# Wide products by S, ten ReLU halves on ScalarE, and a new hand-written order in an attention-then-routing kernel

## The chip, the cores and the metric

The kernel runs on one core of one Trainium2 chip. The metric is the device time of the whole launch in microseconds. The core has a matrix engine (PE, with its weight loads shown apart as PEld), a vector engine (DVE), a scalar engine (ACT) and GpSimd (POOL). Each runs its own queue in order. SP issues most of the DMAs, and POOL issues the indirect ones (scatters by a list of row numbers).

## What is computed

Two blocks are joined. The first is an attention without softmax. For each of 4 x 4 batch-heads, with 1088 rows of 32 numbers each, q and k are projected by two 8 x 32 matrices S1 and S2, and the outer product of the two projections (64 numbers) is the feature vector of the row. The second sends each of the 4352 resulting rows of 128 numbers to one of 8 experts.

```
def phi(x):
    a = np.einsum('rd,bhsd->bhsr', S1, x)
    b = np.einsum('rd,bhsd->bhsr', S2, x)
    return np.einsum('bhsi,bhsj->bhsij', a, b).reshape(*x.shape[:-1], r * r)
q_p, k_p = (phi(q), phi(k))
kv = np.einsum('bhsf,bhsd->bhfd', k_p, v)
z = np.sum(k_p, axis=2)
num = np.einsum('bhsf,bhfd->bhsd', q_p, kv)
den = np.einsum('bhsf,bhf->bhs', q_p, z)[..., None] + 1e-06
attn = num / den
...
x = attn.transpose(0, 2, 1, 3).reshape(B * S, H * D)
logits = x @ w_gate
expert_idx = np.argmax(logits, axis=1)
...
for e in range(E):
    mask = expert_idx == e
    h = np.maximum(x[mask] @ w1[e], 0.0)
    out[mask] = gate_w[mask, None] * (h @ w2[e])
```

S1 and S2 come as 64-bit floats. The kernel splits each of their numbers into a high and a low 32-bit part (`s_cat[:, 0]` and `s_cat[:, 1]`), so the projection is the sum of a product by the high part and a product by the low part.

## The kernel before, in words

All arithmetic of the large products is in fp32. The work is written as small named operations, each issuing instructions for mostly one engine, and one string, `ORDER`, lists them: every engine runs its instructions in the order in which this list names them. After the list a loop at the end of the kernel does the tiles that it leaves over. Buffers are handed out from rings while the list is walked, so the list also sets which buffer an operation reuses and whom it waits for.

The attention is cut into chunks of 512 rows of one batch: `k00`, `k01` ... `k31` for k (batch, chunk), `q00` ... `q31` for q, and `kr0`, `kr1`, `qr0`, `qr1` for the remainders (one quarter of the size). A chunk's operations are:

- `.t` four transposes on PE, `.x` ACT copies them out of PSUM, `.a` PE multiplies by S (L359), `.s` ACT copies the projections out of PSUM in another order (L368), `.o` DVE forms the outer products (L378, 128 x 1024 numbers).
- for k: `.v` PE adds the chunk to kv (L387, L391).
- for q: `.T` and `.U` PE transposes the features, `.c` and `.d` ACT copies them, `.n` and `.N` PE multiplies them by kvx (L505, 128 x 82), and DVE divides: `.e`, `.g`, `.y` for the first half of the chunk and `.e2`, `.g2`, `.y2` for the second. `.g` gives logits, `.y` gives rows of x.

`e0` ... `e3` end a batch's kv: `.r` adds the remainder, `.k`, `.t`, `.c`, `.m`, `.z` turn kv into kvx, which the batch's `.n` needs. `r0` ... `r3` route a batch: `.a`, `.b`, `.c`, `.d` on DVE (argmax and ranks, a small PE step `.p` between `.b` and `.d`), and then the scatters `.s0` ... `.s8` on POOL, each of which writes 128 rows into `xs_dram` at their places, sorted by expert. `t0`, `t1` and `t2` compute on DVE which expert and which rows the tiles 0 to 9, 10 to 17 and 18 onwards hold.

A tile `j0`, `j1`, ... is 128 rows of one expert: `.l` SP loads the rows, `.x` PE transposes them, `.c` ACT copies the result, `.w` DVE copies the expert's first weights into a buffer of the `wide` ring (L832), `.u` and `.U` PE multiplies by the two halves of them (L837, 8 instructions each), `.r` ACT does the ReLU of the first half (L854) and `.q` DVE that of the second (L860), `.d` PE multiplies by the second weights (L869, 16 instructions), `.y` ACT scales, `.s` POOL scatters the rows to the output. Tiles 0 to 9 may be loaded once the scatters of batches 0 and 1 have landed, tiles 10 to 17 once those of batch 2 have, the rest after batch 3. In this run 37 tiles are computed: 34 always, and 3 of the 7 that stand under conditions near the end.

Of the kernel before, what the change touches and what calls it, by code (L numbers as in the profile page):

```python
# [12 lines left out]
AF = mybir.ActivationFunctionType  # L13
ALU = mybir.AluOpType
# [3 lines left out]


ORDER = """  # L20
k00.t k00.x k01.t S.t k01.x S.m k00.a kr0.t k01.a k00.s kr0.x k00.o kr0.a k01.s kr0.s kr0.o k00.v k01.o q00.t
q01.t q00.x k01.v q01.x k10.t q01.a k10.x k10.a q01.s q01.o k11.t k10.s q00.a k11.x k10.o k11.a q00.s q00.o
k10.v k11.s e0.r q01.U e0.k k11.o q00.U q01.d e0.t q00.d q00.T e0.m e0.c e0.z q01.T q00.c q00.N q01.c q01.N
q00.e2 q00.y2 q01.n q00.g2 q01.e2 q01.g2 q01.y2 q00.n q01.e q01.y k21.t q00.e k11.v q01.g k21.x q00.g q00.y
q11.t r0.a k21.a q11.x r0.b r0.x q11.a k21.s r0.c e1.r k21.o q11.s qr0.t r0.p e1.k qr0.x q11.o e1.t qr0.a e1.c
q10.t qr0.s e1.m r0.d k20.t q10.x q11.T k20.x q10.a e1.z r0.s2 qr0.o q11.c q11.U q10.s qr0.T r0.s1 q10.o q11.d
q11.n qr0.c q11.N q11.e r0.s6 q11.g q11.y q10.T q11.e2 q10.U q10.c q11.y2 qr0.n r0.s4 q11.g2 q10.d q10.n qr0.e
qr0.y r0.s7 q10.N qr0.g q10.e q10.y q21.t q10.g q10.e2 k20.a r0.s5 q21.x q10.g2 q10.y2 r1.a q21.a k20.s r0.s0
k30.t k20.o r1.x q21.s q20.t k30.x kr1.t k31.t r0.s3 q20.x r1.b k30.a k31.x r1.c r1.p q21.o k30.s kr1.x q20.a
r1.d q21.T k30.o q20.s r1.s8 q21.U q21.c k20.v q21.d q20.o k30.v r1.s1 k21.v t0.a k31.a r1.s2 t0.b q20.T k31.s  # L30
q20.U q20.c k31.o kr1.a r1.s5 q30.t q20.d qr1.t q31.t kr1.s q30.x t0.c k31.v qr1.x r1.s0 q31.x kr1.o q30.a
j0.w e2.r r1.s3 q30.s qr1.a j1.w e2.k e3.r qr1.s e2.t e3.k j2.w q31.a r1.s4 e2.c e2.m qr1.o e3.t q31.s e2.z
qr1.T q30.o r1.s6 e3.c q21.n qr1.c q20.n e3.m t0.d r1.s7 q21.e q20.N e3.z q21.g q21.y q20.e q21.N q31.o qr1.n
q20.y q30.T q20.e2 q30.U q21.e2 q30.c j3.l q20.y2 q31.T q21.g2 q30.d q21.y2 q30.n q20.g2 j0.l q31.c qr1.e
q20.g q30.N qr1.g r2.a j4.l q31.n q30.e r2.x j1.l r2.b q31.U r2.c r2.p q31.d j2.l q30.y q30.g j0.x q30.e2
q31.N j0.c r2.d j0.u q30.y2 r2.s2 t1.a j1.x j0.U j0.r q30.g2 t1.b j1.c r2.s7 j1.u j5.l j0.q j3.x t1.c j2.x
j1.r j0.d r2.s4 j3.c j3.w j2.c r2.s1 t1.d j1.U j0.y qr1.y q31.e j2.u j0.s q31.e2 j6.l j1.q j4.x j4.w j2.U j2.r
r2.s3 j4.c j1.d q31.y2 j7.l j5.w r2.s6 j2.q j5.x j3.u q31.g j1.y q31.g2 q31.y r2.s5 j5.c r3.a j2.d j3.r j1.s
r3.b r3.x r3.c r3.p j2.y r2.s0 j3.U r3.d j2.s j4.u j3.q j8.l j6.w j6.x j3.d j4.r r3.s7 j6.c t2.a r3.s1 j5.u
t2.b j3.y j4.U j5.r r3.s6 j6.u t2.c j9.l j7.x r3.s4 j5.U j6.r j4.q j7.c j6.U j10.l j5.q r3.s3 j7.w j4.d j11.l  # L40
j9.w r3.s5 j9.x j6.q j8.x j4.y j5.d j9.c r3.s0 j8.c j8.w t2.d r3.s8 j7.u j5.y j6.d j7.r r3.s2 j7.U j3.s j6.y
j8.u j12.l j7.q j6.s j10.w j10.x j7.d j8.r j10.c j4.s j9.u j7.y j5.s j8.U j9.r j9.U drain j13.l j8.q j11.w
j11.x j8.d j11.c j14.l j9.q j12.w j12.x j10.u j8.y j12.c j9.d j10.r j11.u j9.y j7.s j10.U j11.r j9.s j12.u
j13.w j15.l j13.x j11.U j12.r j10.q j8.s j13.c j12.U j14.w j16.l j13.u j12.q j17.l j11.q j14.x j15.x j13.U
j14.c j15.c j15.w j14.u j18.l j16.w j10.d j14.U j13.q j13.r j10.y j18.o j11.d
"""
AFTER_LATE = "k11.o"
PREPARE = (18, 19, 20, 21, 23, 24, 27)
# [6 lines left out]
def kernel(  # L55
# [21 lines left out]
    JC = 4  # L77
# [23 lines left out]
    def new(name, shape, dtype=FP):  # L101
        return sb.tile(shape, dtype, name=name)
# [14 lines left out]
    def ring(name, n, shape, dtype=FP):  # L117
        return Ring([new(f"{name}{i}", shape, dtype) for i in range(n)])
# [2 lines left out]
    wide = ring("wide", WIDE, [128, 1024])  # L121
    xT_bufs = ring("xT", 3, [128, 512])
    sum_bufs = ring("sum", 4, [128, 2 * JC * H * R])
    q_pT_bufs = ring("q_pT", 5, [128, 512])
    kvz_bufs = ring("kvz", 2, [128, 96])
    xg_bufs = ring("xg", 14, [128, XW])
    xgT_bufs = ring("xgT", 7, [128, 128])
    hTa_bufs = ring("hTa", 3, [128, HF])
    hTb_bufs = ring("hTb", 3, [128, HF])
    to_bufs = ring("to", 14, [128, 1], I32)  # L130
    y_bufs = ring("y", 12, [128, DM])
    xs_dram = dram.tile([(E + 1) * NTOK, XW], I32, name="xs_dram")


# [75 lines left out]
    for b in range(B):  # L210
        t = new(f"x_rows{b}", [128, J + 1, XW])
# [57 lines left out]
    s_cat = new("s_cat", [128, 2, 2, 4, R])  # L269
# [41 lines left out]
    def hold(t, n):  # L311
        holders[id(t)] = [t, n]
# [26 lines left out]
    def features(x, n, srcs, take_dst, keeps):  # L339
        st = {}  # L340

        @op(x + ".t")
        def _():
            t = st["tp"] = banks.take()
            for i, s in enumerate(srcs()):
                nc.tensor.transpose(t[:, ts(i, 128)], in_=s, identity=ident)  # L346

        @op(x + ".x")
        def _():
            st["xT"] = xT_bufs.take()  # L350
            nc.scalar.copy(out=st["xT"][:, :n * 128], in_=st["tp"][:, :n * 128])  # L351
            banks.give(st["tp"])

        @op(x + ".a")
        def _():
            t = st["ab"] = banks.take()
            for i in range(n):
                for part in range(2):
                    nc.tensor.matmul(t[:, ts(i, 64)], lhsT=st["xT"][:, ts(i, 128)],  # L359
                                     rhs=s_cat[:, part].rearrange("p t g r -> p (t g r)"),  # L360
                                     start=(part == 0), stop=(part == 1), skip_group_check=True)
            xT_bufs.give(st["xT"])

        @op(x + ".s")
        def _():
            s = st["s"] = sum_bufs.take()
            hold(s, 1 + keeps)
            nc.scalar.copy(out=s[:, :n * 64].rearrange("p (g i r) -> p i g r", i=n, r=R),  # L368
                           in_=st["ab"][:, :n * 64].rearrange("p (i g r) -> p i g r", i=n, r=R))
            banks.give(st["ab"])  # L370

        @op(x + ".o")
        def _():
            s = st["s"]
            st["p"] = take_dst()
            dst = st["p"][:, :n * 4 * RR].rearrange("p (g a b) -> p g a b", a=R, b=R)
            a, b = (s[:, ts(t, n * 32)].rearrange("p (g r) -> p g r", r=R) for t in range(2))
            nc.vector.tensor_tensor(dst, a[:, :, :, None].broadcast_to([128, n * 4, R, R]),  # L378
                                    b[:, :, None, :].broadcast_to([128, n * 4, R, R]), ALU.mult)
            let(sum_bufs, s)  # L380

        return st
# [398 lines left out]
    st = [dict() for _ in range(JT)]  # L781
# [8 lines left out]
    def expert_tile(j):  # L790
        x = f"j{j}"
        s = st[j]

        @op(x + ".l")
        def _():
            s["xg"] = xg_bufs.take()
            r = word(tiles[j][1], [SP], E * NTOK)
            d = nc.sync.dma_start(out=s["xg"].bitcast(I32), in_=xs_dram[ds(r, 128), :])
            g = (j >= JE) + (j >= JF)
            if g not in begun:  # L800
                begun.add(g)
# [55 lines left out]
        @op(x + ".q")  # L857
        def _():
            s["hTb"] = hTb_bufs.take()
            nc.vector.tensor_scalar(s["hTb"], s["hb"], 0.0, None, ALU.max)  # L860
            banks.give(s["hb"])

        @op(x + ".d")
# [112 lines left out]
    def part(js, bit):  # L976
        for j in js:
            st[j]["y"] = y_bufs.take()
        with tc.If(bit > 0):
# [64 lines left out]
```

## Time and profile before

| what | us |
|---|---|
| median of 4 runs | 228.27 |
| runs | 228.01, 232.96, 228.53, 227.22 |
| the profiled execution's own time | 228.01 |
| its span, first to last instruction | 226.2 |
| PE busy / DVE busy / ACT busy / POOL busy | 215.9 / 120.6 / 73.0 / 82.5 |
| first product by S, first transpose of a tile, last product | 9.3, 79.04, 221.9 |

The run's time is 1.8 us longer than the span. In the profile a group is a line of the kernel, an engine and an operation, with its count, its busy time and the mean of one. A PE product's own duration (275 ns) is longer than the distance from one start to the next, because products overlap in the array: what PE can take in is read from the starts in the timeline. One fp32 product of the program is two PE instructions. A wait is put down to what came last.

### The profile page before, as it was taken

Reading aid. Unit: us, or ns where it says so; the run is one execution under the profiler, and the core shown is the slowest. Engines: PE = TensorE matmul, PEld = TensorE weight load, DVE = VectorE, ACT = ScalarE, POOL = GpSimd, SP = SyncE. Lnnn points to the kernel's source line nnn. Section 1 sums busy time; section 2 is a strip of 40 time slices with the busy share of each in tenths; the row PEclk is TensorE's granted clock in tenths of the full one; section 3 lists DMA queues with packets and bytes.
Section 4 is the critical chain, followed back from the end, with each engine's and each line's share of the span. In section 5 each row is a group of like instructions: output and inputs, shape, how many; then the busy total and the mean of one; then the engine's idle time right before and its main releaser. Section 6 shows DMA issues by size and latency. Waiting matters only on the chain. (4 is left out here: it accounts for less than half of the span.)

```text
span 226.2 us, 6247 instructions
## 1 busy us (share of the span) xinstructions
PE 215.9 (95%) x2245; PEld 211.6 (94%) x2245; DVE 120.6 (53%) x389; ACT 73.0 (32%) x190; POOL 82.5 (36%) x103
## 2 busy tenths in 40 slices
PE   6999999999999999997999999999999699999992
PEld 5889999999999999997999999999999699999991
DVE  4244678587678999989652422425344343323220
ACT  2243524524452332331323222332323223132320
POOL 5100000871781056777615033222222234117133
PEclk9999999999999999999999999999999999999998
DMA  5999999998112211152121112111010110000000
GB/s 163 286 348 247 251 297 345 337 346 264 45 46 60 64 47 47 61 118 63 47 61 35 35 38 59 39 35 51 15 44 26 47 33 16 10 3 32 25 25 15
DMA packets 29279, 23.33 MB, mean 103 GB/s; under 512 B 5866, under 2 KB 27116, under 8 KB 29248
## 3 DMA queue, kind: packets, MB, share of 16 engines
q1 hardware_dynamic: 26304, 18.15, 28.8%
q0 software_dynamic: 2400, 4.50, 5.6%
q8 instruction: 20, 0.33, 0.6%
q10 hardware_dynamic: 544, 0.26, 0.4%
q14 instruction: 11, 0.09, 0.1%
HBM read 17.81 MB, written 5.55 MB: 103 GB/s over the span
## 5 line engine op out<-in xcount | busy, mean ns | idle before, releaser
L837 PE MATMUL bank<-xgT,wide 128*128 128x128 f32 x592 | 72.2, 275 | 0.0
L837 PEld LDWEIGHTS bank<-xgT,wide 128*128 128x128 f32 x592 | 69.1, 192 | 0.0
L860 DVE TENSOR_SCALAR hTb<-bank 128x512 f32<-128x512 f32 x37 | 25.3, 688 | 67.3 <-PE bank L837 54.6
L616 POOL DMA_INDIRECT xs_dram<-x_rows,row_i x34 | 37.7, 1107 | 55.6 <-DVE kvx L467 29.1
L869 PE MATMUL bank<-w_all,hTb 128*128 x296 | 39.3, 276 | 1.2 <-DVE hTb L860 1.2
L883 POOL DMA_INDIRECT out_dram<-y,to x23 | 23.0, 1000 | 47.5 <-ACT xgT L825 32.8
L869 PE MATMUL bank<-w_all,hTa 128*128 x296 | 39.3, 276 | 0.0
L869 PEld LDWEIGHTS bank<-w_all,hTb 128*128 128x128 f32 x296 | 36.0, 192 | 1.4 <-DVE hTb L860 1.4
L869 PEld LDWEIGHTS bank<-w_all,hTa 128*128 128x128 f32 x296 | 36.0, 192 | 0.2
L878 ACT ACTIVATE y<-bank,xg 128x128 f32<-128x128 f32 x37 | 13.6, 367 | 65.9 <-PE bank L869 65.9
L359 PE MATMUL bank<-s_cat,xT 128*128 128x64 f32 x272 | 32.8, 275 | 0.4 <-DVE s_cat L332 0.4
L359 PEld LDWEIGHTS bank<-s_cat,xT 128*128 128x128 f32 x272 | 31.5, 192 | 0.9 <-issue 0.5
L854 ACT ACTIVATE hTa<-bank 128x512 f32<-128x512 f32 x37 | 22.1, 597 | 28.2 <-PE bank L837 22.6
L883 POOL DMA_INDIRECT out_dram<-y,xg x18 | 18.0, 1000 | 31.3 <-ACT y L878 17.9
L832 DVE COPY wide<-w_all 128x1024 f32 x39 | 27.2, 708 | 1.7 <-issue 1.6
L378 DVE TENSOR_TENSOR wide<-sum 128x1024 f32<-128x1024 f32 (+1 forms) x18 | 20.4, 1132 | 11.6 <-ACT sum L368 11.5
L505 PE MATMUL bank<-kvx,q_pT 128*128 128x82 f32 x128 | 15.4, 276 | 0.3 <-ACT q_pT L493 0.3
L505 PEld LDWEIGHTS bank<-kvx,q_pT 128*128 128x128 f32 x128 | 14.8, 192 | 0.6 <-ACT q_pT L493 0.5
L368 ACT COPY sum<-bank 128x256 f32<-128x256 f32 (+1 forms) x20 | 6.8, 341 | 24.7 <-PE bank L359 23.4
L351 ACT COPY xT<-bank 128x512 f32<-128x512 f32 (+1 forms) x20 | 9.9, 527 | 12.6 <-PE bank L346 11.5
L493 ACT COPY q_pT<-bank 128x512 f32<-128x512 f32 (+1 forms) x18 | 9.4, 566 | 7.3 <-PE bank L485 7.1
L825 ACT COPY xgT<-bank 128x128 f32<-128x128 f32 x41 | 10.0, 263 | 5.2 <-PE bank L820 4.9
(153 smaller groups left out, 160.6 us busy)
## 6 DMA issues: line engine op xcount, KB each, us to landing
w_all<-in_moe_w_dram SPq DMA_DIRECT2D x16, 512.0 KB, 8.7
xg<-xs_dram SPq DMA_DIRECT2D x41, 65.0 KB, 1.8
wide<-in_v_dram SPq DMA_DIRECT2D x4, 512.0 KB, 5.6
wide<-in_q_dram SPq DMA_DIRECT2D x4, 512.0 KB, 8.6
wide<-in_k_dram SPq DMA_DIRECT2D x3, 512.0 KB, 7.9
xs_dram<-fill SPq DMA_DIRECT2D x1, 585.0 KB, 11.0
xs_dram<-x_rows,row_i POOLq DMA_INDIRECT x34, 2.9
out_dram<-y,to POOLq DMA_INDIRECT x23, 2.2
```

The costliest lines, as they stand in the source:

```text
L359: nc.tensor.matmul(t[:, ts(i, 64)], lhsT=st["xT"][:, ts(i, 128)], rhs=s_cat[:, part].rearrange("p t g r -> p (t g r)"), start=(part == 0), ...
L378: nc.vector.tensor_tensor(dst, a[:, :, :, None].broadcast_to([128, n * 4, R, R]), b[:, :, None, :].broadcast_to([128, n * 4, R, R]), ALU.mult)
L505: nc.tensor.matmul(o, lhsT=lhsT, rhs=kvx[b][:, hp].rearrange("p g c -> p (g c)"), start=True, stop=True)
L616: d = nc.gpsimd.indirect_dma_start(out=xs_dram[:], out_offset=bass.IndirectOffsetOnAxis(ap=st["row"][:, u:u + 1], axis=0), in_=x_rows[b][: ...
L825: nc.scalar.copy(out=s["xT"], in_=s["tp"][:, :128])
L832: nc.vector.tensor_copy(out=s["w1"], in_=w1_all[:, ds(r, F)])
L837: nc.tensor.matmul(t[:, ts(c, 128)], lhsT=s["w1"][:, ts(c0 + c, 128)], rhs=s["xT"], start=True, stop=True)
L854: nc.scalar.activation(s["hTa"], s["ha"], AF.Relu)
L860: nc.vector.tensor_scalar(s["hTb"], s["hb"], 0.0, None, ALU.max)
L869: nc.tensor.matmul(t[:, :DM], lhsT=h[:, ts(c % 4, 128)], rhs=w2_all[:, ds(r + c * DM, DM)], start=(c == 0), stop=(c == 7))
L878: nc.scalar.activation(s["y"], s["py"][:, :DM], AF.Copy, bias=0.0, scale=s["xg"][:, DM:DM + 1])
L883: d = nc.gpsimd.indirect_dma_start(out=out[:], out_offset=bass.IndirectOffsetOnAxis(ap=s["to"](), axis=0), in_=s["y"], in_offset=None, bou ...
```

## The change

Four things change.

- `.a` multiplies each transposed block once by the high and low part side by side (128 columns) instead of twice by 64 columns with accumulation. The low half of the result goes to its own columns in PSUM.
- The two halves are added on DVE. A new operation `.l` of a chunk copies the low half out of PSUM on ACT into a buffer `lo`, of which there is one; `.s`, now on DVE, adds the high half from PSUM to it and writes the sum in the order that the ACT copy used before.
- `.q` is on ACT for tiles 0 to 9 (JE is 10), and on DVE for the others as before.
- `ORDER` is a new list. The rings `xg` and `y` have one buffer less each. The loop at the end, with its conditions, is as it was.

```diff
-    xg_bufs = ring("xg", 14, [128, XW])
+    lo_bufs = ring("lo", 1, [128, JC * H * 2 * R])
+    xg_bufs = ring("xg", 13, [128, XW])
...
-    y_bufs = ring("y", 12, [128, DM])
+    y_bufs = ring("y", 11, [128, DM])
...
             for i in range(n):
-                for part in range(2):
-                    nc.tensor.matmul(t[:, ts(i, 64)], lhsT=st["xT"][:, ts(i, 128)],
-                                     rhs=s_cat[:, part].rearrange("p t g r -> p (t g r)"),
-                                     start=(part == 0), stop=(part == 1), skip_group_check=True)
+                nc.tensor.matmul(t[:, ts(i, 128)], lhsT=st["xT"][:, ts(i, 128)],
+                                 rhs=s_cat.rearrange("p w t g r -> p (w t g r)"), start=True, stop=True)
             xT_bufs.give(st["xT"])
+
+        def part(i):
+            return st["ab"][:, :n * 128].rearrange("p (i w c) -> p i w c", i=n, w=2)[:, :, i]
+
+        @op(x + ".l")
+        def _():
+            st["lo"] = lo_bufs.take()
+            nc.scalar.copy(out=st["lo"][:, :n * 64].rearrange("p (i c) -> p i c", i=n), in_=part(1))
 
         @op(x + ".s")
         def _():
             s = st["s"] = sum_bufs.take()
             hold(s, 1 + keeps)
-            nc.scalar.copy(out=s[:, :n * 64].rearrange("p (g i r) -> p i g r", i=n, r=R),
-                           in_=st["ab"][:, :n * 64].rearrange("p (i g r) -> p i g r", i=n, r=R))
+            nc.vector.tensor_tensor(
+                s[:, :n * 64].rearrange("p (g i r) -> p i g r", i=n, r=R),
+                part(0).rearrange("p i (g r) -> p i g r", r=R),
+                st["lo"][:, :n * 64].rearrange("p (i g r) -> p i g r", i=n, r=R), ALU.add)
             banks.give(st["ab"])
+            lo_bufs.give(st["lo"])
...
             s["hTb"] = hTb_bufs.take()
-            nc.vector.tensor_scalar(s["hTb"], s["hb"], 0.0, None, ALU.max)
+            if j < JE:
+                nc.scalar.activation(s["hTb"], s["hb"], AF.Relu)
+            else:
+                nc.vector.tensor_scalar(s["hTb"], s["hb"], 0.0, None, ALU.max)
             banks.give(s["hb"])
```

Of the new list, the stretch around the first tile's load reads as follows (`...` leaves out what lies before and behind):

```
...
q21.g2 q21.g q21.y q30.U r1.s4 r1.s3 q31.d q31.N q20.g2 r2.a r2.b j1.w q30.d q31.n r1.s2 q31.e q31.g q31.y
q30.c j0.w qr1.n q30.N r2.p r1.s8 r1.s1 r2.d r2.x q31.e2 q31.y2 r1.s0 q31.g2 qr1.e qr1.g j0.l r2.c j0.x q30.n
j0.c j1.l j1.x j1.c r2.s3 j0.u j0.U j2.l j0.r r2.s5 j0.q j2.x j2.w r2.s2 qr1.y j3.l j3.x j3.c j4.l j2.c j1.u
...
```

and that in the list before:

```
...
q20.g q30.N qr1.g r2.a j4.l q31.n q30.e r2.x j1.l r2.b q31.U r2.c r2.p q31.d j2.l q30.y q30.g j0.x q30.e2
q31.N j0.c r2.d j0.u q30.y2 r2.s2 t1.a j1.x j0.U j0.r q30.g2 t1.b j1.c r2.s7 j1.u j5.l j0.q j3.x t1.c j2.x
...
```

More of the change, by code (lines that the diff above doesn't have):

```diff
@@ L20 @@
 ORDER = """
[L21 to L45, printed above, removed]
+k00.t k00.x k01.t S.t S.m k00.a kr0.t k01.x k00.l k00.s k00.o kr0.x k01.a k01.l k01.s kr0.a k01.o q01.t q01.x
@@ new lines @@
+q00.t k00.v kr0.l kr0.s kr0.o q00.x q01.a q01.l q01.s q01.o k11.t k11.x k01.v e0.r k10.t q00.a e0.k e0.t e0.m
+e0.z k10.x q00.l q00.s q00.o q10.t k10.a q10.x e0.c k11.a k10.l k10.s k10.o q01.T q01.c q10.a q10.l qr0.t
+q10.s q10.o q01.U q01.d q00.T q00.c q01.n q01.e k11.l q01.y q00.U k11.s q21.t q00.n q00.e qr0.x qr0.a k11.o
+q00.d q00.y q01.N qr0.l q00.N qr0.s q21.x q11.t q21.a k10.v k11.v q00.e2 e1.r q11.x q20.t q00.g2 qr0.o q21.l
+q01.e2 q01.g2 q01.g q00.g r0.a q21.s r0.x q11.a q10.U k20.t r0.b r0.p q01.y2 e1.k e1.t q00.y2 r0.c q11.l k20.x
@@ new lines @@
+q10.d qr0.T q11.s q11.o k20.a r0.d r0.s2 r0.s6 q20.x r0.s4 q10.T r0.s7 q11.U e1.c e1.m e1.z q11.T q21.o q10.N
+k20.l k20.s k20.o q10.e2 q10.c q10.n q10.y2 q11.c q10.e r0.s0 q10.g q11.n q11.e q11.g q10.g2 qr0.c qr0.n qr0.e
+r0.s1 qr0.g q11.d q11.N k21.t k21.x kr1.t q10.y kr1.x q11.e2 q11.g2 r1.a r1.b r0.s3 q11.y2 r1.x q20.a k30.t
+q20.l k20.v q30.t qr0.y r1.p q11.y r1.c kr1.a q30.x q20.s r1.d r1.s7 r1.s5 q20.o k30.x k21.a k21.l k21.s k31.t
+r0.s5 k21.o kr1.l k31.x kr1.s kr1.o q21.U q21.d q31.t qr1.t t0.a t0.b q30.a k30.a k30.l q31.x k30.s t0.c k30.o
@@ new lines @@
+k21.v e2.r e2.k qr1.x k31.a k31.l q20.U q20.d q21.T e2.t e2.m q31.a qr1.a e2.z k31.s k31.o q20.T e2.c q31.l
+q31.s q31.o r1.s6 q21.N q21.e2 q21.c q20.N qr1.l qr1.s qr1.o k30.v k31.v q20.e2 e3.r q20.y2 q20.c e3.k q31.T
+q31.U q21.y2 q30.l q30.s q20.n q31.c q30.o e3.t e3.c e3.m e3.z qr1.T qr1.c q21.n q20.e q20.g q30.T q20.y q21.e
+q21.g2 q21.g q21.y q30.U r1.s4 r1.s3 q31.d q31.N q20.g2 r2.a r2.b j1.w q30.d q31.n r1.s2 q31.e q31.g q31.y
+q30.c j0.w qr1.n q30.N r2.p r1.s8 r1.s1 r2.d r2.x q31.e2 q31.y2 r1.s0 q31.g2 qr1.e qr1.g j0.l r2.c j0.x q30.n
@@ new lines @@
+j0.c j1.l j1.x j1.c r2.s3 j0.u j0.U j2.l j0.r r2.s5 j0.q j2.x j2.w r2.s2 qr1.y j3.l j3.x j3.c j4.l j2.c j1.u
+j1.U j1.r j4.x j4.c j2.u j1.q q30.e2 j2.r q30.e j2.U j3.w j3.u j4.w j0.d j0.y j1.d j5.w q30.y q30.g j5.l j5.x
+q30.g2 r3.a r3.b j5.c j4.u j4.r j4.U j3.r j3.U j6.w j0.s t0.d t1.a t1.b j5.u t1.c r2.s4 j2.q j6.l j6.x r2.s6
+j7.w j1.y j1.s j3.q r2.s7 j2.d j3.d j5.r j5.U j8.l q30.y2 j8.x j8.w j6.c j6.u j3.y j3.s j6.U j7.l j9.w j7.x
+j4.q j4.d j5.q j9.l r2.s1 t1.d r2.s0 j10.l j6.q j9.x j7.c j7.u j7.U j9.c r3.x j2.y j11.l r3.p j5.d j6.r r3.c
@@ new lines @@
+j6.d r3.d t2.a j7.r j7.q t2.b j2.s r3.s1 r3.s7 j10.w j8.c j8.u j8.r j8.U j11.x j10.x j10.c t2.c j9.u j9.r t2.d
+j11.w j5.y r3.s5 j5.s j8.q j9.U j12.w j9.q j12.l j10.u j7.d r3.s4 j13.l j12.x j10.U j10.q j10.r j12.c j15.l
+j8.d j11.c j4.y j14.l j11.u j13.x j11.r j12.u j13.w j12.U j15.w j11.U j14.x r3.s2 j13.c j6.y j14.c j17.l j9.d
+j13.u j9.y j10.d j12.q j6.s r3.s3 j12.r j13.r r3.s0 drain j7.y j7.s j15.x j14.w j15.c j11.q j11.d j14.u j12.d
+j14.r j14.U j17.x j16.l j14.q j17.c j13.U j15.u j15.U r3.s8 r3.s6 j13.q j20.l j16.x j16.c j11.y j12.y j16.w
@@ L46 @@
+j11.s j13.d j13.y j15.r j14.d
 """
```

## The prediction

> **What bounds the kernel now.** I read the page's busy shares and groups first, then PE's waits, then the timelines of PE and DVE around the places that the change touches.
>
> ```profile
> PE 215.9 (95%) x2245; PEld 211.6 (94%) x2245; DVE 120.6 (53%) x389; ACT 73.0 (32%) x190; POOL 82.5 (36%) x103
> PE   6999999999999999997999999999999699999992
> DVE  4244678587678999989652422425344343323220
> L359 PE MATMUL bank<-s_cat,xT 128*128 128x64 f32 x272 | 32.8, 275 | 0.4 <-DVE s_cat L332 0.4
> L368 ACT COPY sum<-bank 128x256 f32<-128x256 f32 (+1 forms) x20 | 6.8, 341 | 24.7 <-PE bank L359 23.4
> ```
>
> PE is busy from end to end and waits for almost nothing; what it waits for by name is 6.4 us in all, the longest of it these three:
>
> ```profile
> PE bank L820 <- PEq L979: 1.7, 1, 1.7
> PE bank L869 <- DVE hTb L860: 1.2, 1, 1.2
> PE bank L224 <- DVE zeros L169: 1.1, 1, 1.1
> ```
>
> So a microsecond of PE work removed ahead of the last product is worth about one microsecond, if the other engines can follow. The second row of digits says where that is in doubt: DVE is at six to nine tenths in the stretch in which the products by S stand (9.3 to 69.3 us).
>
> What PE pays for one instruction is the distance between starts:
>
> ```profile
> 16.64 3.68 PE L359 MATMUL bank<-s_cat,xT 128*128 128x64 f32 x32
> 20.16 0.61 PE L346 MATMUL bank<-ident,wide 128*128 128x128 f32 x4
> ...
> 63.98 2.00 PE L359 MATMUL bank<-s_cat,xT 128*128 128x64 f32 x16
> 65.91 0.32 PE L387 MATMUL bank<-k_rem_p,v_rem 64*32 64x64 f32 x8
> ...
> 190.72 3.74 PE L837 MATMUL bank<-xgT,wide 128*128 128x128 f32 x32
> 194.29 1.06 PE L869 MATMUL bank<-w_all,hTa 128*128 x8
> ```
>
> 32 products of 64 columns take 20.16 - 16.64 = 3.52 us, 110 ns each; in the worse group 16 take 1.93, 121 ns. 32 of 128 columns take 194.29 - 190.72 = 3.57, 112 ns each. The width costs nothing between 64 and 128.
>
> **The change, part by part.** *The wide product.* 272 instructions become 136. Before: 272 x 110 to 272 x 121, 29.9 to 32.9; I take 114 (most groups lie at 110 to 114), 31.0. After: 136 x 112 = 15.2. PE loses 14.7 to 17.7 us of work; I take 15.5.
>
> The Trainium skill speaks against this one: "TensorE: Matmul & The Clock Gate", in the steps of Part 2, has a stream of matmuls cost one cycle per moving column, N/2.4 + 2.5 ns, which I estimate at 29 ns for 64 columns and 56 for 128. By that the wide product would cost nearly what the two narrow ones did, and the gain would be under 1 us. The same page says that a stream of weight load and matmul pairs is spaced by both; the rows here (110 against 112 ns) agree with that and not with the first rule.
>
> *The low copy.* `.l` takes the place of the old `.s` on ACT: 20 copies out and 20 in, of the same size (341 ns). Nothing is added to ACT's sum.
>
> *The add on DVE.* 16 of 128 x 256 and 4 of 128 x 64. No such row exists; nearest are the division L532 (128 x 256, one input from PSUM), which starts its successor 0.33 to 0.34 us later, and L378 at 128 x 256, up to 0.47 long. Lower end 16 x 0.33 + 4 x 0.14 (L526 by starts) = 5.8 us, upper 16 x 0.47 + 4 x 0.21 = 8.4. I take 6.1, by starts, since DVE's queue is full there.
>
> *The ten ReLU halves.* 10 x 0.69 (L860) leave DVE and 10 x 0.60 (L854) come to ACT, 6.0 us over tiles that hold PE for 10 x 3.7 us, with ACT at a third. On ACT `.r`, `.q`, `.c` and `.y` of a tile make 0.60 + 0.60 + 0.26 + 0.37 = 1.8 of 3.7. I cost it at nothing. What hides it is this half; uncovered it would be 0.6 per tile, 6.0.
>
> *The new order.* Here I made a running sum: in each list I added, operation by operation, what each puts on its engine, by the starts in the timeline (`.t` 0.52, old `.a` 1.79 and new 0.89, `.v` 0.65, `.T` 0.48, `.n` 0.90, `.u` 0.89, `.d` 1.79 on PE; `.s` 0.35, `.o` 1.09, a half's division 0.31 + 0.14 + 0.33, a route 3.2 on DVE). In the old list PE's sum ahead of `j0.x` is 71.1, and `j0.x` started at 79.04: PE began 8.0 us into the span and lost nothing net. DVE's old sum between `t0.d` and `t2.d` is 36.8; the trace has 107.12 - 70.70 = 36.4. So the sums can be trusted to some 2%.
>
> In the new list PE's sum ahead of `j0.x` is 55.8, so it stands at 8.0 + 55.8 = 63.8 if nothing is late. Then what is late:
>
> - DVE. It must have done 52.3 us of work by the end of `j0.w`. It can't start the first divisions before PE has done `q00.n`, at 24.9, when its own sum is 12.1; from there it has 52.3 - 12.1 = 40.2 to do and ends at 24.9 + 0.2 + 40.2 = 65.3, and PE wants `j0.w` for `j0.u` at 64.9. The two meet to within half a microsecond, and so they do at `q21.N` (its kvx ready at 53.0, wanted at 52.5) and `k21.v` (47.8 against 47.7). Elsewhere the lead is 0.1 us or more. I take 0.6 us of PE idle, and 0.6 more for handovers at the front that the sum doesn't hold. If each add costs the upper end, 2.3 us more come by then.
> - ACT's leads over PE, summed in the same way, are 0.3 to 4 us up to the first tile: nothing.
> - POOL. `j0.l` now stands behind all 17 scatters of batches 0 and 1. The trace has 39.52 to 50.45 for the first 8 and 55.85 to 69.06 for the next 9, 24.1 in all; the first can start after `r0.d`, which DVE ends at 35.0. With a gap of 0.5 before the second batch's they end at 60.1. Before, the first tile load was issued 2.3 us after the last scatter it needed began (70.39 - 68.08), and takes 1.8: 59.1 + 2.3 + 1.8 = 63.2, wanted at 63.8. Nothing, by 0.6 us. If every scatter took the longest one's time (1.77 + 0.30), it would be 10.4 us late.
> - SP: behind a late `j0.l` on its queue stand all later tile loads, which wait for the same scatters; the 16 weight loads are ahead of it in the list. The loads of batch 3 are issued earlier than before, since `q00.t` and `k01.v` come sooner.
> - Tiles 10 onwards: DVE waits for `r3.p` at 89.3 and then stands level with PE at `j11.u` (102.2 both). Up to 1 us; I take 0.3.
>
> What goes: the wait of `.d` for `.q` at 102.9 to 104.1 (1.17), caused by the routing and table work on DVE ahead of it. The first ten `.q` have no such queue now. The 1.7 at L979 (the conditions) stays, and so does the end.
>
> **Sum.** 226.2 - 15.5 - 1.2 + 0.6 + 0.6 + 0.3 = 211.0 of span; + 1.8 around it = 212.8, against 228.01 of the profiled run. The median stands 0.26 above that run, so 213.1; I say 213.0.
>
> **Rivals.**
>
> *A, DVE paces the front.* For: DVE sums to PE's own length from 25 to 65 us, and in the old trace DVE waited 11.5 us in 10 places for `sum` of L368 alone, 1.15 each; a chunk's chain now has one hop more. Against: most of those waits stand where DVE was ahead of PE. If half of that returns in the stretch where DVE has no reserve, 5.7 us: 218.7.
>
> *B, the scatters are late.* For: all 17 stand in front of the first tile and there is 0.6 us of reserve. Against: the old trace shows only five of the first 17 above 1.1 us. At 0.25 us more per scatter, 4.3 - 0.6 = 3.7: 216.7.
>
> *C, slower: the single `lo` buffer.* ACT's queue stops at `.l` of a chunk until DVE has done `.s` of the one before, and behind `.l` stand the `.x` and `.c` copies that PE waits for. There are 20 such handovers between 10.5 and 64.9 us, 2.7 us each. One takes 0.34 + 0.35 and what DVE has in front: an outer product (1.1), or a route's `.a` and `.b` (1.8): 1.8 to 2.5 with no hop counted. It decides above 2.7 and makes the kernel slower above 2.7 + 15.5 / 20 = 3.5; at 3.7 the time is 213 + 20 x 1.0 = 233. Against it: the sums have ACT ahead of PE everywhere with this wait counted.
>
> *D, the wide product costs PE twice a narrow one.* Then 15.5 us don't come: 228.5. The rows speak against it.
>
> **How the numbers follow.** Forecast 0.68, A 0.16, B 0.09, C 0.04, D 0.03. What a measurement of this kernel can tell from no change is about 0.5%, 1.1 us. Faster: forecast, A and B and a part of D, 0.94; same 0.02; slower 0.04. The forecast's own terms lie 1.4 lower with the narrow product at 121 ns and no handover lost (2.2 + 0.6, less half since both at once are unlikely), and 2 to 3 higher with the add's upper end. The range reaches from there to A: 210.5 to 219.
>
> **What would show it.** Products by S: 136 at 110 to 114 ns from start to start, PE busy near 200 us. The first transpose of a tile (79.04 before) at 63 to 65; later by more than 1 us means a rival: PE's waits then name `wide`, `sum` or kvx on DVE (A), the tile's load (B), or ACT's xT and q_pT with ACT waiting for DVE's `sum` (C). From there to the last product (142.9 us before) some 141 to 143. DVE's add near 0.41 in duration; above 0.5 the DVE term was too small. I am wrong if PE's waits exceed some 8 us.

## The result, and the profile after

| | before | changed |
|---|---|---|
| median, us | 228.44 (32 runs, 226.52 to 233.25) | 218.49 (22 runs, 214.81 to 220.85) |
| the runs that the ratio compares, their median | 20 runs, 227.98 | 9 runs, 215.02 |
| ratio of these | | 0.945, 95% interval 0.942 to 0.948 |
| the profiled execution, its span | 228.01, 226.2 | 219.95, 218.2 |
| first transpose of a tile, first product by a tile's weights | 79.04, 80.59 | 68.26, 71.05 |
| last product | 221.63 | 213.57 |

The kernel became faster: by 10 us from median to median of all runs, by 13 between the runs that the ratio compares. The forecast was 15 (213.0); the median, 218.49, lies just inside the upper end of the range, 219.0. Executions of one kernel don't all agree (the changed one has 9 runs at 214.8 to 217.0 and 13 at 218.4 to 220.9, the one before 20 up to 229.7 and 12 at 232.6 to 233.3), so the ratios here compare only the lower group of each kernel, while both undisturbed profiles of the changed kernel are of its upper one.

The runs below come from four sittings. In three of them, called disturbed, whole engines stopped for some microseconds at a time (see the last section). Each run is compared with its own sitting, and of the disturbed ones only those parts of a trace are read closely in which no engine stopped.

The page's busy shares, its digits in 40 slices (5.5 us each) and the group of the products by S, of the changed kernel:

```profile
PE 205.0 (94%) x2109; PEld 200.1 (92%) x2109; DVE 121.8 (56%) x399; ACT 77.1 (35%) x200; POOL 83.5 (38%) x103
PE   6999999999897999999969999999999699999992
DVE  4276899999998898428863062353526334232310
PEclk9999999999999699999999999999999999999999
L361 PE MATMUL bank<-s_cat,xT 128*128 128x128 f32 x136 | 20.0, 297 | 0.5 <-DVE s_cat L335 0.5
```

PE has 136 instructions less and 10.9 us less work, but three new dents: slice 11 (8), slice 13 (7) and slice 21 (6). DVE is at nine tenths from slice 6 to slice 12 (27 to 65 us): the reserve it had in the kernel before is gone. And one slice, the 14th, has a granted clock of 0.6, where the kernel before has nine tenths or more in every slice but its last.

What PE waits for, in us, times and longest:

```profile
PE bank L832 <- PEq L994: 1.7, 1, 1.7
PE bank L849 <- DVE hTb L875: 1.7, 1, 1.7
...
PE bank L832 <- DVE x_rows L544: 0.9, 1, 0.9
PE bank L517 <- ACT kvx L465: 0.7, 1, 0.7
PE bank L607 <- DVE oh L593: 0.5, 1, 0.5
...
PE bank L849 <- DVE rk L616: 0.4, 1, 0.4
```

The wait at the conditions (L994, before L979) stayed. The 1.2 that the forecast took off (`.d` for `.q`) came back as 1.7 of a product for `.q` some tiles later. The other four are new, and all four go back to DVE (kvx goes over DVE's reductions to ACT). Each was costed at a fraction of a microsecond or nothing. With the waits at the start (zeros, first load, `s_cat`) all of PE's rows add up to 8.4 us, and to 8.9 in after_b; in the kernel before they add up to 6.1.

The timeline of PE (start, duration, instruction, count) shows the first products by S of this execution:

```profile
9.43 2.05 PE L361 MATMUL bank<-s_cat,xT 128*128 128x128 f32 x8 [0.54 <-DVE s_cat L335]
11.26 0.42 PE L349 MATMUL bank<-ident,k_rem 128*128 128x128 f32 x1
...
14.99 1.16 PE L361 MATMUL bank<-s_cat,xT 128*128 128x128 f32 x8
15.99 0.27 PE L349 MATMUL bank<-ident,wide 128*128 128x128 f32 x1
```

and the same of the second record of the same kernel (after_b, below):

```profile
9.44 1.13 PE L361 MATMUL bank<-s_cat,xT 128*128 128x128 f32 x8 [0.54 <-DVE s_cat L335]
10.41 0.27 PE L349 MATMUL bank<-ident,k_rem 128*128 128x128 f32 x1
```

Eight products take 11.26 - 9.43 = 1.83 us in the first and 10.41 - 9.44 = 0.97 in the second, as they do at 14.99 in the first too. The clock record says why: in the profiled run the clock rose to full at 13.13 us, in the second record at 8.52. The transposes of `q00` stand 1.9 us behind the forecast's running sum in the one (13.82 against 11.93) and 0.1 in the other; the late rise costs some 1.8 us here.

### The profile page after: what moved, and what is told of

It reads as the page before. It is cut to its first block, busy times and chain, and to the rows that moved or that the text cites. A ratio compares the mean times of both kernels' runs of the same rounds, so it can differ in the third digit from the quotient of the medians.

```text
span 218.2 us, 5999 instructions
## 1 busy us (share of the span) xinstructions
PE 205.0 (94%) x2109; PEld 200.1 (92%) x2109; DVE 121.8 (56%) x399; ACT 77.1 (35%) x200; POOL 83.5 (38%) x103
## 5 line engine op out<-in xcount | busy, mean ns | idle before, releaser
L849 PE MATMUL bank<-xgT,wide 128*128 128x128 f32 x592 | 73.6, 279 | 2.1 <-DVE hTb L875 1.7
L849 PEld LDWEIGHTS bank<-xgT,wide 128*128 128x128 f32 x592 | 70.5, 195 | 2.4 <-issue 1.8
L875 DVE TENSOR_SCALAR hTb<-bank 128x512 f32<-128x512 f32 x27 | 18.7, 691 | 61.8 <-PE bank L849 48.9
L898 POOL DMA_INDIRECT out_dram<-y,xg x18 | 18.7, 1039 | 28.9 <-ACT y L893 21.3
L361 PE MATMUL bank<-s_cat,xT 128*128 128x128 f32 x136 | 20.0, 297 | 0.5 <-DVE s_cat L335 0.5
L361 PEld LDWEIGHTS bank<-s_cat,xT 128*128 128x128 f32 x136 | 18.2, 209 | 0.8 <-issue 0.6
L517 PE MATMUL bank<-kvx,q_pT 128*128 128x82 f32 x128 | 16.0, 275 | 0.8 <-ACT kvx L465 0.7
L517 PEld LDWEIGHTS bank<-kvx,q_pT 128*128 128x128 f32 x128 | 15.2, 192 | 1.5 <-ACT kvx L465 0.9
L354 ACT COPY xT<-bank 128x512 f32<-128x512 f32 (+1 forms) x20 | 10.4, 527 | 11.7 <-PE bank L349 11.0
L832 PE MATMUL bank<-ident,xg 128*128 128x128 f32 x41 | 10.2, 276 | 2.6 <-PEq L994 1.7
L349 PE MATMUL bank<-ident,wide 128*128 128x128 f32 x64 | 10.6, 295 | 0.9 <-DMA wide<-in_k_dram 0.9
```

Source lines behind the costliest of these rows:

```text
L361: nc.tensor.matmul(t[:, ts(i, 128)], lhsT=st["xT"][:, ts(i, 128)], rhs=s_cat.rearrange("p w t g r -> p (w t g r)"), start=True, stop=True)
L517: nc.tensor.matmul(o, lhsT=lhsT, rhs=kvx[b][:, hp].rearrange("p g c -> p (g c)"), start=True, stop=True)
L849: nc.tensor.matmul(t[:, ts(c, 128)], lhsT=s["w1"][:, ts(c0 + c, 128)], rhs=s["xT"], start=True, stop=True)
L898: d = nc.gpsimd.indirect_dma_start(out=out[:], out_offset=bass.IndirectOffsetOnAxis(ap=s["to"](), axis=0), in_=s["y"], in_offset=None, bou ...
```

## The experiments

The theories: (1) DVE now paces the end of the front and the stretch around the first tile; (2) the rest is lost behind the front, to the waits above and to the clock; against them the forecast's rivals B (scatters) and C (the single `lo` buffer), and that one part of the change does all or nothing.

### The changed kernel again (after_again, after_b)

No edit; it was run in two sittings as the neighbour of the others.

> The changed kernel once more, for a second profile. In the first one the first transpose of a tile stood at 68.26 us, 4.5 behind the running sum, and the clock was at half until 13.13 and again for 3.41 us from 71.15. Theory: 2.0 us of the 4.5 come from the clock, which rose one window of some 3.4 us later than in the kernel before (9.2), and 2.5 from DVE, late for r1.p and for kvx of batch 2. If the moment at which the clock rises varies from run to run, a profile with an early rise shows the first transpose of a tile at 66 to 67 us. Rival: the late rise belongs to the kernel (its first products are half as many), and every profile of it shows 13 us.

> The changed kernel beside the next three, since in the batch before PE stood still for 4 to 8 us at a time for no releaser between 42 and 67 us, in all four kernels. Without that: first transpose of a tile at 66 to 68 us, last product 145 us later, ratio to the kernel before 0.94 to 0.95. In the batch before, PE was 0.0 us behind the running sum at 30 us and 0.6 at 42 with the clock full from 8.4; theory: here it is again at most 1 us behind at 42 us when the clock rises before 10 us, 2 more when it rises at 13, and falls behind by some 2.5 between 42 and 68, for DVE.

Measured: after_again 240.47 us against 258.57 before, ratio 0.944 (0.931 to 0.958). After_b 218.69 (215.21 to 219.82), with the kernel before at 232.69 (226.36 to 233.28) in that sitting. The ratio of the disturbed sitting agrees with that of the result, so the gain is not a matter of the sitting. The first transpose of a tile stands at 66.61 in after_b, with the clock's rise at 8.52: what after_again's theory expected, and its rival (a late rise in every profile) is out.

After_b is the clean record, and the first tile is read in it. PE:

```profile
66.38 0.19 PE L607 MATMUL bank<-oh,upper 128*128 128x64 bf16 x1
...
66.61 0.31 PE L832 MATMUL bank<-ident,xg 128*128 128x128 f32 x1
...
68.68 0.33 PE L832 MATMUL bank<-ident,xg 128*128 128x128 f32 x1 [0.90 <-DVE x_rows L544]
69.40 3.25 PE L849 MATMUL bank<-xgT,wide 128*128 128x128 f32 x16 [0.40 <-DVE rk L616]
72.44 0.63 PE L832 MATMUL bank<-ident,xg 128*128 128x128 f32 x2
```

The same place in the kernel before:

```profile
79.04 0.31 PE L820 MATMUL bank<-ident,xg 128*128 128x128 f32 x1
...
80.59 1.09 PE L837 MATMUL bank<-xgT,wide 128*128 128x128 f32 x8
```

And DVE beside it in after_b:

```profile
66.10 0.22 DVE L593 TENSOR_TENSOR oh<-cand,first 128x64 bf16<-128x64 f32 x1
67.03 0.69 DVE L844 COPY wide<-w_all 128x1024 f32 x1 [0.70 <-DVE oh L593]
...
68.21 0.41 DVE L544 TENSOR_TENSOR x_rows<-bank,den_q 128x256 f32<-128x256 f32 x1
68.56 0.69 DVE L844 COPY wide<-w_all 128x1024 f32 x1
69.17 0.22 DVE L616 TENSOR_TENSOR rk<-bank,base_e 128x64 f32<-128x64 f32 x1
```

Read from the top: the route `r2` stands in front of the tile. Its small product L607 can start only when DVE has made `oh` (66.10 + 0.22), and the tile's transpose L832 stands right behind it in PE's queue. PE's product ahead of L607 starts at 66.19, and they stand 0.11 apart, so PE would have been ready at 66.30: the two engines arrive there within 0.1 us of each other. The rows had come by then (their load was issued at 64.09, and takes 1.9). What PE lost, it lost further ahead: from 9.44 to 66.61 it is idle for 1.61 us, of which 0.56 before L607 of `r1` at 44.23 and 0.63 before the products with kvx at 55.24.

Behind the first transpose it goes on. DVE's arithmetic stands still for 0.70 before it copies a tile's weights. The profile names `oh`, which had long been done; what fills the time in the trace is DVE's queue loading into a register where the expert's weights lie (L797, 66.11 to 66.66, then the steps that use it), which counts as no busy time and which the running sum didn't hold. The division of x behind that copy gives a bank back late, and the next transpose waits 0.90 for that bank; the first products wait 0.40 for the bank of `r2`'s ranks. From first transpose to first product by weights it takes 2.79 us, against 1.55 in the kernel before. And those 16 products take 3.04 from start to start instead of 1.8: the clock falls to half at 69.96 for 3.41 us.

### Is it DVE? (double_add, double_add_b)

```diff
-            nc.vector.tensor_tensor(
+            for _ in range(2):
+                nc.vector.tensor_tensor(
...
```

The add in `.s` is made twice, with the same result.

> Every add on DVE is done twice, so DVE has 16 x 0.33 to 0.45 plus 4 x 0.14 us more before the first tile, 5.8 to 7.8. Theory (DVE paces the stretch from 25 us to the first tile): the first transpose of a tile moves by 4 to 7 us and the time by as much. Rival (PE or the scatters pace it and DVE has reserve): less than 1.5 us.

> Every add on DVE done twice, beside the changed kernel on one chip. In the batch before, up to 43 us, PE lost 3.2 us against the running sum from 24 us on where the changed kernel lost 0.5; the time said nothing. Theory (DVE paces PE from 25 us to the first tile): first transpose of a tile 4 to 7 us later than in the changed kernel and the time 4 to 7 us longer. Rival (DVE catches up, or the scatters pace): below 2 us.

Measured: double_add 237.92 us, after_again beside it 240.47; the sitting was disturbed. Double_add_b 225.35 (223.44 to 226.82), after_b beside it 218.69: +6.7. Its first tile:

```profile
73.35 0.31 PE L833 MATMUL bank<-ident,xg 128*128 128x128 f32 x1
```

73.35 against 66.61, +6.7, and everything behind it takes what it took (145.4 us to the last product, 145.6 in after_b). The 20 additional adds take 8.1 us from start to start (16 of 0.40 to 0.46, 4 of 0.21 to 0.25). So more than four fifths of what DVE gets as more work ahead of the first tile comes out at the end: DVE paces the front. Already at 43 us PE stands 3.2 us behind the running sum in double_add_b, and 0.5 in after_b. The disturbed pair does not show it in the time.

### What is the new order worth? (old_order, old_order_b)

```diff
-k00.t k00.x ... (the new list)
+k00.t k00.x k01.t S.t k01.x S.m k00.a kr0.t k01.a k00.l k00.s kr0.x k00.o kr0.a k01.l k01.s kr0.l kr0.s kr0.o ...
...
```

The list of the kernel before, with each chunk's `.l` put in front of its `.s`; the wide product, the add on DVE and the ReLU on ACT stay.

> The wide product, the copy, the add and the ReLU on ACT, but in the order of the kernel before, with each copy named just ahead of its add. Theory (the new order is what brings the gain of the wide product to the end): PE waits for adds and outer products that stand close behind, 3 to 8 us slower than the changed kernel. Rival (the order matters little, PE's saved work is all): within 1.5 us of it.

> The new operations in the old order, each copy just ahead of its add. In the batch before PE was 5 us behind the running sum at 38 us where the changed kernel was 0.3 behind. Theory (order): 5 to 9 us longer than the changed kernel, that is 0 to 6 us shorter than the kernel before. Rival: within 2 us of the changed kernel.

Measured: old_order 249.98 us, after_again beside it 240.47, ratio to the kernel before 0.974 (0.956 to 0.992). Old_order_b 218.96 (217.78 to 220.61), after_b 218.69. In the profile of the first PE stands still for 8.3 us at 106 us with no releaser, which after_again does not have, so the undisturbed pair is the one to read. Old_order_b at the first tile:

```profile
74.13 0.31 PE L830 MATMUL bank<-ident,xg 128*128 128x128 f32 x1
...
75.17 1.09 PE L847 MATMUL bank<-xgT,wide 128*128 128x128 f32 x8
```

Its first transpose is 7.5 us later than in after_b, but only 1.04 us lie between it and the first product by weights, the clock stays full there, and there is no wait for `hTb`. From first transpose to last product it needs 140.1 us, after_b 145.6. So in these two records the new order gains 7.5 us at the front and gives 5.5 of them back behind it; of the 2.0 that remain, as much can be due to the clock, which rose at 13.13 in this record and at 8.52 in after_b. The expectation, 5 to 9 us longer, did not come. What the order is worth still depends on the clock: one run of after_b has a mean granted clock of 0.998, too high for a 3.41 us stretch at half, and took 215.21, 2.6 us less than the shortest of old_order_b (217.78). One run is too few to settle it. The old order is not free at the front: PE waits there for outer products (L397 and L495 for `wide`, 2.2 and 1.3 us).

### The single `lo` buffer (lo2)

```diff
-    lo_bufs = ring("lo", 1, [128, JC * H * 2 * R])
+    lo_bufs = ring("lo", 2, [128, JC * H * 2 * R], BF)
```

Two buffers, which fit because they hold the low part in bf16.

> Two lo buffers, in bf16, in place of one in fp32, so that the copy of a chunk no longer waits for the add of the chunk before. Theory (DVE paces; the wait only parks ACT): within 1 us of the changed kernel. Rival (the single buffer holds ACT, and through its copies PE): 1 to 3 us shorter, and the waits of ACT's copy to lo for DVE's sum (4.8 us in the changed kernel's profile) and some of PE's lateness at 42 to 68 us are gone.

Measured: 220.24 us (218.34 to 220.67), after_b 218.69. ACT's waits of the copy to `lo` for DVE's sum (5.0 us in after_b) are gone, and the time is no shorter, so rival C has nothing in it. But PE has a new wait:

```profile
PE bank L832 <- DMA xg<-xs_dram: 1.4, 1, 1.4
```

Here PE came to the first tile 0.3 us earlier and waited 1.4 us for its rows; the transpose started at 67.87. That is not the scatters: the load was issued at 63.88, 0.2 earlier than in after_b. It comes in 16 parts, of which 15 had landed by 65.72 and the last at 67.83, so the load took 3.9 us instead of 1.9. One late part cost more than the reserve. POOL's scatters in after_b:

```profile
46.92 1.71 POOL L628 DMA_INDIRECT xs_dram<-x_rows,row_i  x1 [2.25 <-DVE row_i L622]
...
55.71 1.87 POOL L628 DMA_INDIRECT xs_dram<-x_rows,row_i  x1 [0.31 <-issue]
...
60.77 1.97 POOL L628 DMA_INDIRECT xs_dram<-x_rows,row_i  x1 [0.30 <-issue]
```

The gap before batch 1's scatters is 2.25 us, not 0.5, since `r1` is late on DVE too, and three of them take 1.7 to 2.0 instead of 0.98. The last one starts at 60.77, the forecast had 59.1. Rival B is not what sets the time in after_b, but the rows, at 66.0, are only some half a microsecond ahead of their transpose.

### The ReLU (relu_dve, relu_dve_b)

```diff
-            if j < JE:
-                nc.scalar.activation(s["hTb"], s["hb"], AF.Relu)
-            else:
-                nc.vector.tensor_scalar(s["hTb"], s["hb"], 0.0, None, ALU.max)
+            nc.vector.tensor_scalar(s["hTb"], s["hb"], 0.0, None, ALU.max)
```

> The second ReLU half of tiles 0 to 9 is on DVE again, in the new order. Theory: the front (up to the first tile) stays, and of the 10 x 0.69 us on DVE 0 to 2 us show, where the routing of batches 2 and 3 stands ahead of a ReLU on DVE. Rival (DVE is so late after the front that everything on it counts): 4 to 7 us.

> The second ReLU half of tiles 0 to 9 on DVE again, in the new order, beside the run before. In the batch before it was 5.7 us longer than the changed kernel, but on a disturbed chip. Theory: DVE is behind after the front too, so a ReLU on DVE queues behind divisions and routes: 2 to 6 us longer than the changed kernel. Rival (DVE has room there): below 1 us.

Measured: 246.2 us, after_again beside it 240.47; and 246.3, the run routes beside it 245.1. Both sittings were disturbed. As they stand, the first pair, 5.7 us apart, is what the rival of the first expectation said (4 to 7) and not its theory (0 to 2); the second had no changed kernel beside it. The intervals of the ratios to the kernel before (0.961, 0.950 to 0.972; 0.959, 0.946 to 0.971) overlap with after_again's, 0.931 to 0.958, so the size stays open. What can be read is the wait itself, in the second run:

```profile
PE bank L849 <- DVE hTb L872: 3.7, 1, 3.7
```

3.7 us instead of 1.7 in after_b (1.6 in after_again), at the same place, so the ten ReLU halves on ACT take 2 us off that wait: DVE is behind at that place too, and with the halves on it it is further behind.

### All but the wide product (narrow)

```diff
-                nc.tensor.matmul(t[:, ts(i, 128)], lhsT=st["xT"][:, ts(i, 128)],
-                                 rhs=s_cat.rearrange("p w t g r -> p (w t g r)"), start=True, stop=True)
+                for part in range(2):
+                    nc.tensor.matmul(t[:, ds(i * 128 + part * 64, 64)], lhsT=st["xT"][:, ts(i, 128)],
+                                     rhs=s_cat[:, part].rearrange("p t g r -> p (t g r)"), start=True, stop=True)
```

Two narrow products write the two halves; everything else as changed.

> New order, add on DVE and ReLU on ACT as in the changed kernel, but each half of S in a product of its own of 64 columns, as many as before the change. PE has 136 more instructions at 112 ns, 15.2 us. Theory: part of them fill time in which PE waits for DVE, some 4 to 6 us at the front, so the time is 9 to 12 us above the changed kernel, 227 to 231. Rival (PE paces alone): the full 15 us, 233 or more; rival (the width costs nothing either way): within 2 us.

Measured: 255.0 us (249.88 to 257.93), routes and relu_dve_b beside it 245.1 and 246.3, the kernel before 260.75. The changed kernel was not in this sitting, three of narrow's four runs lie at 254 to 258 and one at 249.9, and its profile has the latest rise of the clock of all (20.91), so the size is rough: some 4 to 10 us are lost with the width. Old_order_b has the wide product without the new order and most of the gain, but also the move of the ReLU halves. Together the two point to the wide product as the larger part; the wide product alone was not run.

### Moving the routes out of the way (routes, routes2)

In both, batch 2's route goes from ahead of the first tile to behind the first tiles' products, and batch 3's exponent (`r3.x`, on ACT) right behind `r3.b`. In routes `r3.p` follows `t1.c`, and in routes2 it waits for the tables `t1` to be done; in both `r3.c r3.d` follow it at once:

```diff
-... q20.g2 r2.a r2.b j1.w ... q30.N r2.p r1.s8 r1.s1 r2.d r2.x ... j0.l r2.c j0.x ... j1.c r2.s3 j0.u ...
+... q20.g2 j1.w ... q30.N r1.s8 r1.s1 ... j0.l j0.x ... j4.w r2.a r2.x r2.b j0.d j0.y j1.d r2.p r2.c r2.d r2.s3 r2.s5 r2.s2 ...
...
-... r3.a r3.b j5.c ... t1.d r2.s0 j10.l j6.q ... j9.c r3.x j2.y j11.l r3.p j5.d j6.r r3.c j6.d r3.d t2.a ...
+... r3.a r3.b r3.x j5.c ... t1.d r2.s0 j10.l r3.p r3.c r3.d j6.q ... j9.c j2.y j11.l j5.d j6.r j6.d t2.a ...
```

(the last line is that of routes2)

> Only the order is changed: the routing of batch 2 (r2.a, r2.x, r2.b, r2.p, r2.c, r2.d and its first scatters) stands behind the first tiles' weight copies instead of ahead of the first tile, and r3.x, r3.p, r3.c, r3.d stand some 40 operations earlier. Theory: PE's waits around the first tile (0.9 for x_rows, 0.4 for rk) come from DVE doing batch 2's routing there, and the 1.7 us at 110 us from r3.p being late on PE, with all of DVE's table work behind it. Then the first products of a tile start at 67 to 68 us instead of 69.4, the half-clock window after them goes in most runs, the 1.7 us wait goes, and the time is 3 to 5.5 us below the changed kernel: ratio to the kernel before 0.93 or less. Rival (DVE's sum counts, wherever its work stands): no change of more than 1 us, the waits only move.

> The order of the changed kernel with two routes moved: batch 2's (r2.a, r2.x, r2.b, r2.p, r2.c, r2.d and its first scatters) from ahead of the first tile to behind the tile's first 32 products, as in the run routes, and batch 3's only a little: r3.x right behind r3.b on ACT, and r3.p, r3.c and r3.d as soon as DVE has done t1.d, so that nothing of the tables t1 stands between r3.p and r3.d. Theory (the gain that was lost behind the front went to route and table work that stands too close to PE's turn): the first product of a tile by its weights starts 1.0 to 1.2 us behind the first transpose instead of 2.8, PE's waits for x_rows and rk there are gone, the wait of the hidden-half products for DVE's hTb near 110 us (1.7) is gone, and no wait takes its place; if the clock holds behind the first tile too, the products L849 of the first two tiles have no window at half clock. Together 3.0 to 5.5 us under the changed kernel: 213 to 216 us, a ratio of 0.925 to 0.94 to the kernel before. Rival 1 (the time is set elsewhere, by DVE's sum or the loads): waits of the same size come up behind, and the ratio stays at 0.940 to 0.950. Rival 2 (the half clock comes from something else than the idle moments): the waits go, but a window of 3.4 us at half clock still stands within 5 us of the first tile; then 2 to 3.5 us are gained.

Measured: routes 245.13 us, ratio 0.946 (0.915 to 0.976); routes2 243.06 us, ratio 0.946 (0.934 to 0.958). Both sittings were disturbed. The first tile in routes2:

```profile
83.60 0.27 PE L832 MATMUL bank<-ident,xg 128*128 128x128 f32 x1
...
84.67 1.95 PE L849 MATMUL bank<-xgT,wide 128*128 128x128 f32 x16
```

1.07 us from transpose to product instead of 2.79, no wait for `x_rows` or for `rk`, the clock full for the next 24 us. The same in routes (1.08). But in routes the other move went too far:

```profile
104.28 2.08 PE L884 MATMUL bank<-w_all,hTa 128*128 x8 [4.98 <-DVE base_e L618]
```

`r3.p`'s bank is given back by `r3.d` on DVE, which stood behind three steps of `t1`, and PE waited 4.98 us for that bank. In routes2 this wait is gone, and of the wait for `hTb` 0.3 of 1.7 are left. In their place came waits for `xgT` (0.65), `rk` (0.51) and `lgh` (0.42). From the first tile on PE waits 3.8 us by name instead of 5.2 in after_again, but in idle moments without a releaser 5.4 instead of 4.0 (2.1 of them between 105 and 108 us, where after_again has none), and from first transpose to last product it took 154.3 us against 152.9: the time shows no gain. The ratio, 0.946, is what routes2's first rival expected (0.940 to 0.950), not the theory (0.925 to 0.94). So what causes these waits is shown, in that moving the routes takes them away; that they cost the kernel its time is not shown, since other idle moments came in their place, and neither run was made in an undisturbed sitting.

## Why the prediction was right, and where it was too low

The direction was right, and so was the main term, the wide product. The median came 5.5 us above the forecast, the runs that the ratio compares 2.0 (215.0), for terms of the sum that were too small and some that were missing.

By its own signs the prediction was at its edge. The first transpose of a tile came more than 1 us later than 63 to 65, and PE's waits, 8.4 and 8.9 us, are just past the 8 at which it called itself wrong. The sign is that of rival A, and in kind A is right: double_add_b shows that DVE paces the front. In size it is not: A put 5.7 us there, and the front of after_b is 1.6 us late. That the median, 218.49, falls on A's 218.7 is luck, since most of after_b's lateness lies behind the front, where A had none.

- *The wide product (15.5).* Right. By starts, and with the waits behind them, 272 narrow ones took 31.0 us, as the forecast had it; 136 wide ones 16.3 in after_b and 18.0 in the profiled run, against 15.2. The median spacing is 112 ns in both kernels. The missing 1.1 and 2.8 are the slow clock at the start and short waits, not the width. The first of the two rules cited in the prediction, a cost by moving column, does not hold here; rival D is out.
- *The add on DVE (6.1, up to 8.4).* Durations as forecast, 0.41. By starts too small: the row that it was taken from (0.33 to 0.34) was a division followed by something else, and most adds are followed by the outer product that reads them, in after_b:

```profile
20.18 0.42 DVE L377 TENSOR_TENSOR sum<-bank,lo 128x256 f32<-128x256 f32 x1
20.63 1.23 DVE L390 TENSOR_TENSOR wide<-sum 128x1024 f32<-128x1024 f32 x1
```

  0.45 from start to start. Where an add is followed by something that doesn't read it, it is 0.33. Twelve of the 16 large adds are followed by their reader: 12 x 0.12 = 1.4 us more on DVE, which double_add_b showed to be on the path.
- *"DVE ... meet to within half a microsecond ... I take 0.6 us", and 0.6 for handovers.* Too small, in the direction of rival A: the first transpose came at 66.61 instead of 65.0. The places were one of those named (kvx at `q21.N`, 0.63) and `oh` before `r1.p` (0.56); at the first tile itself the two engines met, as forecast.
- *From the first tile to the end.* The step "From there to the last product some 141 to 143" failed. It took 145.3 and 145.6; with the old order 140.1. The running sum looked at each engine's work, but the moment behind the first transpose was not looked at: a register load, a weight copy and a division stand on DVE between the first two transposes, a second weight copy and a route's last steps ahead of the first products, and the division and the route each hold a bank that PE wants next. +1.75 us against old_order_b, and the half clock right behind it, 1.7 more for PE itself (half of 3.41).
- *"DVE waits for `r3.p` at 89.3 and then stands level with PE at `j11.u` ... I take 0.3."* It was 1.7. What was overlooked is `r3.x`: it stands late in ACT's queue, and DVE waits for it with the tables `t2` behind it, as the timeline of DVE in after_b shows:

```profile
94.08 0.23 DVE L599 TENSOR_REDUCE se<-ex 128x9 f32<-128x72 f32 x1 [5.92 <-ACT ex L583]
...
95.66 0.23 DVE L616 TENSOR_TENSOR rk<-bank,base_e 128x72 f32<-128x72 f32 x1 [0.89 <-PE bank L609]
```

  5.92 + 0.89 us in which DVE did nothing, then 13 us of tables and weight copies, and behind them the ReLU that PE needs at 108.6. In routes2, where `r3.x`, `r3.p` and `r3.d` come earlier, 0.3 is left of that wait.
- *The ReLU on ACT (0).* Right: in both undisturbed profiles no product waited for one of ACT's.
- *Scatters (nothing, by 0.6 us).* Right by a hair, and by luck: they were 1.7 late, and PE was late for DVE as well. (The terms given, 35.0 + 24.1 + 0.5, make 59.6 and not 60.1.)
- *The clock* has no term in the forecast. It is some 1.8 us at the start of the profiled run (a late rise), nothing there in after_b, and 1.7 behind the first tile in both, as far as PE's own products go. The runs without a trace say that more goes with it. Eight of the 22 have a mean granted clock of 0.998 or 0.999 and took 214.8 to 216.8 us (median 215.0); fourteen have 0.991 or 0.992, lower by about what one stretch of 3.41 us at half makes of a span of 217 (0.008), and took 217.0 to 220.9 (median 220.0). Late rise and half clock together would explain 3.5 of these 5 us. No undisturbed trace of the eight was kept, so what the rest is stays open.
- *Smaller slips.* DVE's digits in the stretch of the products by S are 2 to 8, and below 6 up to 23 us, not six to nine tenths throughout; PE's waits in the kernel before add up to 6.1 by the rows, not 6.4; and the forecast's own terms, 1.4 lower, reach down to 211.6, not to 210.5.

| after_b's span, from the forecast's | us |
|---|---|
| forecast | 211.0 |
| first transpose 66.61 instead of 65.0 | +1.6 |
| 2.79 instead of 1.04 up to the first product by weights | +1.75 |
| half clock, half of 3.41 | +1.7 |
| wait for `hTb`, 1.68 instead of 0.3 | +1.4 |
| sum | 217.45 |
| measured | 216.8 |

The rows add up to 0.65 too much. They hold for this execution alone: the eight runs above have spans of 213.0 to 215.0, and the three rows without the half clock would already make 215.75, so in most of those runs not all three can be that large. In the profiled run the first transpose comes 1.65 later, at 68.26, which is the late rise, and its span is 218.2.

## What to carry to other kernels

When the busiest engine is relieved by moving work to one that had reserves, look where that reserve lay: here DVE was at 56% over the whole span and had none in the first 67 us, so 6.7 of 8.1 us added there came out at the end. A running sum by engine finds the places where two engines meet, but here a PSUM bank is given back by the engine that reads it last, so beside every short step of another engine that stands among the products, ask whose bank it holds and what is queued in front of its reader, register loads included. And split a change into its parts on the chip: here the parts without the new order gave most of the gain, and a new order of some 500 operations gained 7.5 us in one place and lost 5.5 in the next.

## What was not expected of the hardware

- *The clock rises at a different moment in each execution of the same kernel, and this costs up to 2 us.* It rose to full at 13.13 us in the profiled run, at 8.52 in after_b and at 8.43 in after_again; among the other kernels it was between 3.94 (double_add) and 20.91 (narrow). The 2 us are the difference between old_order_b's runs at a mean clock of 0.998 (219.84 and 220.61; 13.13 in the one profiled) and at 1.0 (217.78 and 218.09), and the 1.8 above. At half clock 8 products of 128 columns took 1.83 us, 229 ns each, and in narrow 16 of 64 columns 3.44 us (9.27 to 12.71), 215 ns each. So the width is free at half clock too, and the spacing doubles with the clock.
- *It falls again in multiples of 3.41 us behind short pauses, but not behind all.* The clock record of after_b has one such window at 69.96, that of after at 71.15, double_add_b at 76.80, lo2 at 69.61, each behind the stretch around the first tile, in which PE was busy for some 0.6 of 3.41 us. In after_again the same stretch (busy 0.62) was followed by full clock, and so was the wait for `hTb` in those four (busy 0.51). The Trainium skill ("TensorE: Matmul & The Clock Gate", Part 1) has the clock fall after an idle window of about 3.4 us, and has the window run freely, so that the count of slow products differs from run to run. The second agrees with the records. The first does not fit them: the longest pause of PE in the stretches ahead of a fall was 0.9 us in three of the four and 1.4 in lo2, shorter than the 1.7 of the wait for `hTb`. What decides is open.
- *Some sittings stop whole engines.* In five of the eight profiles of the three disturbed ones, ACT stands still for 8.6 us somewhere between 35 and 48 us and DVE for 2.0 to 2.8, with no releaser on the core, PE waits some 4 of it, and the clock falls to half behind it. The other three have stops of ACT of 3 to 10 us. ACT in routes2:

```profile
47.47 0.75 ACT L354 COPY xT<-bank 128x512 f32<-128x512 f32 x2 [8.62 <-remote]
```

  The kernel before lost as much in those sittings (258.6 to 260.8 us instead of 228 to 233), though no profile of it was taken there, and none of the runs tells where it comes from.
